# One PSUM bank shared by three tiles, one mask product per chunk, ReLU on ScalarE, and a third expert buffer

## The chip, the cores and the metric

The kernel runs on one core of a Trainium2 chip. The metric is device microseconds for one execution. An execution is timed several times, and one further execution is profiled.

## The reference

The kernel computes three layers in float32 one after the other.

```
linear attention   4 batches, 8 heads, 768 steps, head width 48
    y[t]  = r[t] (state + u k[t] v[t]^T);   state = w state + k[t] v[t]^T
soft MoE           3072 tokens x 384, 8 experts with 4 slots each, hidden 1024
    logits = x phi;  d = softmax over tokens;  slots = d^T x
    slots of expert e:  max(slot w1[e], 0) w2[e];   out = softmax over slots (logits) @ slot_out
feed-forward       3072 tokens x 384, hidden 2048
    h = x w_in;  g = ELU(h);  out = g w_out
```

## The kernel before

The order of the instructions on each engine is the order in which the program is written (a manual schedule); semaphores are set by a layer that tracks tiles, and for PSUM it treats two accesses of one tile in one bank as dependent even where their columns differ, if they come from different engines.

**Attention.** The 3072 tokens are cut into 24 chunks of 128 (six per batch). The loop at L888 runs s from -2 to 23 and works on four chunks at once: chunk s+1 gets its state update `update` (TensorE, into `pu`), its scores `scores` (16 products into two PSUM tiles `ps_a`, one for each half of the heads), the causal mask product `causal` (VectorE, two instructions of 128x512, one ahead of and one behind the product `rT` of `turn_r`), and its bonus term (`bonus_a` into `ps_b`, `bonus_c` a ScalarE copy, `bonus_b` a transpose into `ps_c`, `bonus_d` the ScalarE copy `bs`). Chunk s gets its output rows `rows_a`, `rows_b` and the transpose `x_T` into `ps_x`. Chunk s+2 gets `turn_k`: four transposes into `ps_k`, a ScalarE copy to `kT`, and later the VectorE product `qd` (`cross`). Chunk s+3 gets `turn_r`: four transposes into `ps_r`, then the VectorE product `rT`. At the end of a step `before` (L637) multiplies the running state into `py`, except for the first chunk of a batch (s = 5, 11, 17).

The 8 banks of PSUM are dealt to pools (L406): `pt` 2 (for `ps_r`, `ps_x`, `ps_k`, in this order in each step), `pa` 2, `py` 1, `pu` 1, `pm` 2 (for `ps_b`, `ps_c`, and the MoE's `ps_l`, `ps_e`, `ps_s`). Between these, `extra()` (three per step) runs one stage of the MoE's logits and slot sums for each four chunks, and `wide_a` to `wide_d` turn pieces of the feed-forward weights from 64 to 32 bits in the steps s = 0 to 19.

**Transfers.** Nearly all are issued by SyncE in program order: in each step the next k and v rows, a piece of the wide weights, every second step r, and, every 20/9 steps from s = 2 on, one expert weight (1.5 MB in four transfers, `load_we`). v of a chunk has four buffers; `update` is the first to read it.

**End of attention and experts.** `last_part` (L773) ends the slot sums: `ps_e` transposes, the VectorE copy `et`, the sums `ps_s`, the VectorE products `pl`, the TensorE products `pi`, and `si`, the slots' input. Then `up` (48 products, ReLU by VectorE at L1052), `turn` (transposes into `ph` buffers, copied by ScalarE to `h1T`), `turn_c_a` and `turn_c_b` (the combine weights, split into two parts and transposed), `down`, and `turn_so`. Expert weights 11 and 12 are loaded into room that attention leaves, 13 to 15 into buffers that `up(0)` leaves. Then the feed-forward layer runs to the end, in 48 units.

Of the kernel before, what the change touches and what calls it, by code (L numbers as in the profile page):

```python
# [236 lines left out]
def kernel(  # L237
# [156 lines left out]
    si = const.tile([128, KD, 32], F32, name="si")  # L394
# [3 lines left out]
    with ExitStack() as actx:  # L398
# [164 lines left out]
        pu = pu_p.tile([128, HP, D], F32, name="pu")  # L563
        nc.vector.memset(pu, 0.0)

# [11 lines left out]
        def scores(n, p):  # L577
            if p == 0:
                aps[:] = [pa_p.tile([128, HP, 128], F32, tag="pa", name="ps_a") for a in range(2)]
            for a in range(2):  # L580
                q = slice(64 * a, 64 * a + 64)
                nc.tensor.matmul(out=aps[a][:, p, :], lhsT=kT[q, p, :], rhs=rT[n][q, p, :], start=True, stop=True)  # L582

        def causal(n, a):
            am[n, a] = at2.tile([128, HP, 128], F32, tag="am", name="am", bufs=3)
            nc.vector.tensor_tensor(  # L586
                out=am[n, a], in0=aps[a], in1=mask.unsqueeze(1).to_broadcast([128, HP, 128]), op=ALU.mult
            )
# [29 lines left out]
        def bonus_b(n):  # L618
            pb = pm_p.tile([128, 128], F32, tag="pm", name="ps_c")
# [31 lines left out]
        def rows_a(n, p):  # L651
            c, py = n % NC, pyd[n]
            for a in range(2):
                h = 2 * p + a

                for q in range(0, C, 64):
                    nc.tensor.matmul(  # L657
                        out=py[q:q + 64, h, :], lhsT=am[n, a][:, p, q:q + 64], rhs=vd[n][:, h, :],
                        start=(c == 0), stop=(c == 0 or h == H - 1),
                    )  # L660
            if p == HP - 1:
                am.pop((n, 0)), am.pop((n, 1))
# [225 lines left out]
        for s in range(-2, NCH):  # L888
# [42 lines left out]
            if nxt:  # L931
                causal(s + 1, 1)
# [46 lines left out]
    mid = main.enter_context(tc.tile_pool(name="mid", bufs=1, reuse_waits="tile"))  # L979
# [22 lines left out]
    rm = ea.tile([128, NCH // CG, CG], F32, name="rm")  # L1002
    rs = ea.tile([128, NCH // CG, CG], F32, name="rs")
# [19 lines left out]
    sel = ea.tile([128, 2, NS], F32, name="sel")  # L1023
# [15 lines left out]
    so = [ea.tile([128, DM], F32, name=f"so{a}") for a in range(2)]  # L1039

    def up(a):
        for f in range(2):
# [9 lines left out]
            nc.vector.tensor_scalar(out=h1[a, f], in0=ph, scalar1=0.0, scalar2=None, op0=ALU.max)  # L1052
# [11 lines left out]
    def down(a):  # L1064
        po = po_p.tile([128, DM], F32, tag="po", name="pd")
        for j in range(KF):
            for q in range(4):
# [3 lines left out]
                )  # L1071
        for kk in range(KD):
# [69 lines left out]
    sT = mid.tile([128, KD, 64], F32, name="sT")  # L1142
# [323 lines left out]
```

## Time and profile before

| what | us |
|---|---|
| three timed runs | 440.98, 440.31, 435.86 |
| their median | 440.31 |
| the profiled execution, timed | 437.81 |
| its span from first to last instruction | 435.7 |
| attention (to the first `up` product) | 0 to 163.0 |
| experts (to the end of `turn_so`) | 163.0 to 189.0 |
| feed-forward | 189.0 to 435.7 |

In the profiled execution 2.1 us lie outside the span. TensorE is busy for 93% of the span, VectorE for 82%, ScalarE for 62%, GpSimd for 37%. In the rows, PE is TensorE's products and PEld its weight loads, DVE is VectorE, ACT ScalarE, POOL GpSimd; "L533" is a line of the kernel; a bracket at the end of a row tells how long its engine had been idle and whose work ended that. A release is inferred from semaphores.

### The profile page before, as it was taken

What the parts mean: (1) busy time and instruction counts of PE and PEld (TensorE: products, weight loads), DVE (VectorE), ACT (ScalarE), POOL (GpSimd) and SP (SyncE); (2) the same over time, 40 slices, a digit from 0 to 9 for tenths busy, and PEclk for the clock granted to TensorE, in tenths of its full rate; (3) what the DMA queues carried; (4) which work ended last, traced back from release to release, by engine and by line L of the source; (5) the groups of instructions that cost most, each with busy time, mean ns of one, the idle gap of its engine ahead of it and who ended that gap; (6) DMA issues with size and microseconds to landing.
All of it is one profiled execution on the core that took longest, in us unless ns stands there. A gap on an engine that the chain in (4) does not pass through costs nothing.

```text
span 435.7 us, 10350 instructions
## 1 busy us (share of the span) xinstructions
PE 405.5 (93%) x4177; PEld 356.0 (82%) x4177; DVE 357.9 (82%) x573; ACT 269.8 (62%) x496; POOL 160.2 (37%) x170
## 2 busy tenths in 40 slices
PE   6998999799999979988999999999999899999994
PEld 5777778587777853457999999998989889999994
DVE  5898999969999645669889999998988989777762
ACT  3554566546564411647697878776778767767750
POOL 2265666546666207200004513430314125433340
PEclk9999999989999999999999999999999999999998
DMA  8969998999999986900001111110111002111122
GB/s 149 232 159 278 253 240 274 279 286 247 283 298 257 353 281 219 360 5 0 2 0 38 37 38 37 37 42 32 38 36 38 0 2 72 63 48 47 63 74 80
DMA packets 85097, 57.44 MB, mean 132 GB/s; under 512 B 65328, under 2 KB 76848, under 8 KB 85040
## 3 DMA queue, kind: packets, MB, share of 16 engines
q1 hardware_dynamic: 84224, 56.64, 45.1%
q8 instruction: 35, 0.57, 0.5%
q14 instruction: 22, 0.18, 0.1%
q10 hardware_dynamic: 816, 0.05, 0.1%
HBM read 51.96 MB, written 4.72 MB: 130 GB/s over the span
## 4 chain that ended last, share of the span: by engine, by line
PE 67%; DVE 20%; ACT 5%; issue 5%; DMA 2%; DVEq 0%; ACTq 0%; SPq 0%
PE fo L1304 12%; PE fo L1307 12%; PE fo L1305 12%; PE ps_a L582 4%; PE fh L1259 4%; PE py L657 4%; DVE rT L547 3%; DVE ex L1273 3%; DVE ex L1278 2%; PE pd L1068 2%; PE ph L1046 2%; PE py L643 2%; DVE am L586 2%; PE ps_k L533 2%; PE ps_r L533 2%
## 5 line engine op out<-in xcount | busy, mean ns | idle before, releaser
L1304 PE MATMUL fo<-wh,gh 128*128 128x384 f32 x384 | 130.3, 339 | 1.5 <-ACT gh L1286 1.0
L1305 PE MATMUL fo<-wl,gh 128*128 128x384 f32 x384 | 129.7, 338 | 0.0
L1307 PE MATMUL fo<-wh,gl 128*128 128x384 f32 x384 | 125.5, 339 | 3.2 <-DVE gl L1289 3.2
L1273 DVE SCALAR_TENSOR_TENSOR ex<-ex,th 128x1024 f32<-128x1024 f32 (+1 forms) x52 | 61.1, 1174 | 20.5 <-ACT ex L1270 20.3
L1304 PEld LDWEIGHTS fo<-wh,gh 128*128 128x128 f32 x384 | 72.1, 188 | 6.0 <-ACT acc L1241 2.4
L1307 PEld LDWEIGHTS fo<-wh,gl 128*128 128x128 f32 x384 | 71.8, 188 | 4.2 <-DVE gl L1289 4.2
L1267 ACT ACTIVATE th<-fh 128x1024 f32<-128x1024 f32 (+1 forms) x53 | 50.3, 950 | 38.3 <-PE fh L1259 38.3
L1305 PEld LDWEIGHTS fo<-wl,gh 128*128 128x128 f32 x384 | 72.1, 188 | 1.8
L1289 DVE TENSOR_TENSOR gl<-ex,gh 128x1024 fp32r<-128x1024 f32 (+1 forms) x52 | 68.3, 1314 | 1.7 <-ACT gh L1286 1.3
L337 POOL TENSOR_TENSOR cv<-raw,cv 128x384 f32<-128x384 f32 x12 | 19.4, 1618 | 132.4 <-ACT gh L1286 51.2
L1278 DVE SCALAR_TENSOR_TENSOR ex<-ex,fh 128x1024 f32<-128x1024 f32 (+1 forms) x52 | 58.8, 1131 | 0.5 <-ACT ex L1270 0.4
L1270 ACT ACTIVATE ex<-fh 128x1024 f32<-128x1024 f32 (+1 forms) x53 | 50.3, 949 | 9.6 <-DVE gl L1289 9.2
L1286 ACT CAST gh<-ex 128x1024 fp32r<-128x1024 f32 (+1 forms) x52 | 51.4, 988 | 6.3 <-DVE ex L1278 4.9
L1246 POOL TENSOR_TENSOR acc<-os,acc 128x384 f32<-128x384 f32 x20 | 27.0, 1361 | 43.7 <-ACT os L1245 43.7
L631 POOL TENSOR_TENSOR bv<-vd,bs 128x384 f32<-128x384 f32 x24 | 24.5, 1021 | 39.6 <-ACT bs L626 38.9
L586 DVE TENSOR_TENSOR am<-ps_a,mask 128x512 f32<-128x512 f32 x48 | 32.5, 680 | 2.0 <-PE ps_a L582 1.9
L1259 PE MATMUL fh<-cT,mst 128*128 128x512 f32 x96 | 30.5, 398 | 1.8 <-DVE mst L1186 1.1
L582 PE MATMUL ps_a<-rT,kT 64*128 64x128 f32 x384 | 28.3, 288 | 0.3 <-ACT kT L556 0.3
L657 PE MATMUL py<-vd,am 128*64 128x48 f32 x768 | 27.7, 226 | 0.4 <-DVE am L586 0.4
L657 PEld LDWEIGHTS py<-vd,am 128*64 128x64 f32 x768 | 25.4, 142 | 0.9 <-DVE am L586 0.7
L556 ACT COPY kT<-ps_k 128x512 f32<-128x512 f32 x24 | 14.1, 586 | 18.8 <-PE ps_k L533 18.8
L582 PEld LDWEIGHTS ps_a<-rT,kT 64*128 64x128 f32 x384 | 23.8, 190 | 1.7 <-ACT kT L556 0.4
(166 smaller groups left out, 650.9 us busy)
## 6 DMA issues: line engine op xcount, KB each, us to landing
we<-in_moe_w_dram SPq DMA_DIRECT2D x14, 768.0 KB, 7.6
we<-in_moe_w_dram SPq DMA_DIRECT2D x16, 512.0 KB, 6.4
rw<-in_r_dram SPq DMA_DIRECT2D x12, 384.0 KB, 5.0
rk<-in_k_dram SPq DMA_DIRECT2D x24, 192.0 KB, 4.8
vd<-in_v_dram SPq DMA_DIRECT2D x24, 192.0 KB, 5.4
out_dram<-acc SPq DMA_DIRECT2D x24, 192.0 KB, 1.9
we<-in_moe_w_dram SPq DMA_DIRECT2D x16, 256.0 KB, 5.9
scr<-in_moe_w_out_dram SPq DMA_DIRECT2D x10, 384.0 KB, 5.9
```

The source lines that it names most:

```text
L582: nc.tensor.matmul(out=aps[a][:, p, :], lhsT=kT[q, p, :], rhs=rT[n][q, p, :], start=True, stop=True)
L657: nc.tensor.matmul(out=py[q:q + 64, h, :], lhsT=am[n, a][:, p, q:q + 64], rhs=vd[n][:, h, :], start=(c == 0), stop=(c == 0 or h == H - 1),)
L1259: nc.tensor.matmul(out=ph[n][:, i, :], lhsT=mst[(f + i) // 8][:, 128 * ((f + i) % 8):128 * ((f + i) % 8) + 128], rhs=cT[:, TB * blk:TB * b ...
L1267: nc.scalar.activation(out=th[n][:, s], in_=ph[n][:, s], func=ACTF.Tanh, scale=0.5)
L1270: nc.scalar.activation(out=ex[n][:, s], in_=ph[n][:, s], func=ACTF.Exp)
L1273: nc.vector.scalar_tensor_tensor(out=ex[n][:, s], in0=ex[n][:, s], scalar=1.0, in1=th[n][:, s], op0=ALU.add, op1=ALU.mult)
L1278: nc.vector.scalar_tensor_tensor(out=ex[n][:, s], in0=ex[n][:, s], scalar=0.0, in1=ph[n][:, s], op0=ALU.min, op1=ALU.max)
L1286: nc.scalar.copy(out=gh[n][:, s], in_=ex[n][:, s])
L1289: nc.vector.tensor_tensor(out=gl[n][:, s], in0=ex[n][:, s], in1=gh[n][:, s].bitcast(F32), op=ALU.subtract)
L1304: nc.tensor.matmul(out=o, lhsT=gh[n][:, i, s], rhs=wh, start=(f == first), stop=False)
L1305: nc.tensor.matmul(out=o, lhsT=gh[n][:, i, s], rhs=wl, start=False, stop=False)
L1307: nc.tensor.matmul(out=o, lhsT=gl[n][:, i, s], rhs=wh, start=False, stop=(f == final))
```

## The change

Seven edits, of which the first three belong together:

- PSUM is dealt anew: `pt` 3 banks, `pa` one tile of 2 banks, `py` 1, `pm` 1, and one bank `pub` that holds `pu` (columns 0 to 191), `ps_b` (192 to 319) and `ps_c` (320 to 447).
- `causal` becomes one VectorE instruction of 128x1024 over both halves of the heads, ahead of `rT`; its result has one buffer in place of three.
- The tables `pw` and `vk` lie in buffers of `rT` and `qd`.
- `load_we` starts at s = 1 in place of 2, so the weights 0 to 8 are issued one step earlier.
- Small tiles (`si`, `rm`, `rs`, `sel`, `sT`, `so`) lie in tiles that are done with, and behind attention there is room for three expert weights (11, 12 and 13) in place of two.
- ReLU goes from VectorE to ScalarE.
- `up(1)` is written ahead of `turn_c_a(0)`.

```
-        pt_p = actx.enter_context(tc.tile_pool(name="pt_p", bufs=2, space=PSUM))
-        pa_p = actx.enter_context(tc.tile_pool(name="pa_p", bufs=2, space=PSUM))
+        pt_p = actx.enter_context(tc.tile_pool(name="pt_p", bufs=3, space=PSUM))
+        pa_p = actx.enter_context(tc.tile_pool(name="pa_p", bufs=1, space=PSUM))
...
-        pm_p = actx.enter_context(tc.tile_pool(name="pm_p", bufs=2, space=PSUM))
+        pm_p = actx.enter_context(tc.tile_pool(name="pm_p", bufs=1, space=PSUM))
...
-        pu = pu_p.tile([128, HP, D], F32, name="pu")
+        pub = pu_p.tile([128, 512], F32, name="pub")
+        pu = pub[:, 0:HP * D].rearrange("p (h d) -> p h d", d=D)
         nc.vector.memset(pu, 0.0)
+        psb, psc = pub[:, 192:320], pub[:, 320:448]
...
-        def causal(n, a):
-            am[n, a] = at2.tile([128, HP, 128], F32, tag="am", name="am", bufs=3)
+        def causal(n):
+            am[n] = at2.tile([128, 2, HP, 128], F32, tag="am", name="am", bufs=1)
             nc.vector.tensor_tensor(
-                out=am[n, a], in0=aps[a], in1=mask.unsqueeze(1).to_broadcast([128, HP, 128]), op=ALU.mult
+                out=am[n].rearrange("p a h t -> p (a h) t"), in0=aps[0].rearrange("p a h t -> p (a h) t"),
+                in1=mask.unsqueeze(1).to_broadcast([128, H, 128]), op=ALU.mult,
             )
...
-            pb = pm_p.tile([128, 512], F32, tag="pm", name="ps_b")
+            pb = psb
...
-            pb = pm_p.tile([128, 128], F32, tag="pm", name="ps_c")
+            pb = psc
...
-                causal(s + 1, 0)
+                causal(s + 1)
...
-            if nxt:
-                causal(s + 1, 1)
...
-            if s >= 2 and (s - 2) * (NWE - 1) // NP >= nwe and nwe < NWE - 1:
+            if s >= 1 and (s - 1) * (NWE - 1) // NP >= nwe and nwe < NWE - 1:
...
-    for i in range(nwe, nwe + 2):
-        load_we(i, we2b_p)
+    for i in range(nwe, nwe + 3):
+        load_we(i, we2b_p[i - nwe])
...
-            nc.vector.tensor_scalar(out=h1[a, f], in0=ph, scalar1=0.0, scalar2=None, op0=ALU.max)
+            nc.scalar.activation(out=h1[a, f], in_=ph, func=ACTF.Relu)
...
+    up(1)
     turn_c_a(0)
-    up(1)
```

Three places in the order of the engines. First TensorE in one step of attention, from `ps_r` to the next chunk's state update; before:

```order
L533 MATMUL ps_r<-ident,rp 128x128 [waits PE_49,Activation_49]
L533 MATMUL ps_r<-ident,rp 128x128 x3
L676 MATMUL ps_x<-ident,x 128x128 [waits DVE_49]
L676 MATMUL ps_x<-ident,x 128x128 x2
L620 MATMUL ps_c<-ident,bt 128x128 [waits Activation_49]
L533 MATMUL ps_k<-ident,km 128x128 [waits DVE_49]
L533 MATMUL ps_k<-ident,km 128x128 x3
L643 MATMUL py<-qb_149,rT 64x96 [waits Pool_49]
L643 MATMUL py<-qb_149,rT 64x96 x7
L569 MATMUL pu<-vd,km 48x48 [waits DMAHW7_49]
L569 MATMUL pu<-vd,km 48x48 x7
```

The same place now:

```order
L679 MATMUL ps_x<-ident,x 128x128 [waits DVE_49]
L679 MATMUL ps_x<-ident,x 128x128 x2
L623 MATMUL pub<-ident,bt 128x128 [waits Activation_49]
L533 MATMUL ps_k<-ident,km 128x128 [waits PE_49]
L533 MATMUL ps_k<-ident,km 128x128 x3
L646 MATMUL py<-qb_148,rT 64x96 [waits PE_49,Pool_49]
L646 MATMUL py<-qb_148,rT 64x96 x7
L571 MATMUL pub<-vd,km 48x48 [waits DMAHW7_49,Activation_49]
L571 MATMUL pub<-vd,km 48x48 x7
```

`ps_k` no longer waits for VectorE (its buffer's last reader before was `rT` of the same step), and the state update `pub<-vd,km` now also waits for ScalarE, whose last access of the bank is the copy `bs` out of `ps_c`.

Second, TensorE in `last_part`, from the first `ps_e` transpose to `pi`; before:

```order
L723 MATMUL ps_e<-ident,el 128x128 [waits Activation_49]
L424 MATMUL warm<-ident 128x128 [waits PE_49]
L424 MATMUL warm<-ident 128x128
L739 MATMUL ps_s<-x,et 32x384 [waits DVE_49]
L739 MATMUL ps_s<-x,et 32x384 x3
L723 MATMUL ps_e<-ident,el 128x128 [waits Activation_49]
L424 MATMUL warm<-ident 128x128 x2
L807 MATMUL pi<-rb,pl_2852 128x32 [waits DVE_49]
L807 MATMUL pi<-rb,pl_2853 128x32 [waits DVE_49]
L807 MATMUL pi<-rb,pl_2854 128x32 [waits DVE_49]
```

The same place now:

```order
L726 MATMUL ps_e<-ident,el 128x128 [waits PE_49,Activation_49]
L424 MATMUL warm<-ident 128x128 x2
L742 MATMUL ps_s<-x,et 32x384 [waits DVE_49]
L742 MATMUL ps_s<-x,et 32x384 x3
L726 MATMUL ps_e<-ident,el 128x128 [waits DVE_49,PE_49]
L424 MATMUL warm<-ident 128x128 x2
L810 MATMUL pi<-rb,pl_2731 128x32
L810 MATMUL pi<-rb,pl_2732 128x32
L810 MATMUL pi<-rb,pl_2733 128x32
```

With one `pm` bank the first `ps_e` takes the bank of `ps_l`, whose last reader is the ScalarE copy `el` (`slots_g`), and the second takes that of `ps_s`, whose last reader is the third `pl` product on VectorE; `pi`, behind it, has no wait left of its own.

Third, ScalarE behind attention, from the exponentials of the combine weights on; before:

```order
L1010 ACTIVATE c_sb<-c_sb 128x256 [waits Pool_49] x3
L1120 TENSOR_LOAD flag_i [waits DVE_49]
L1080 CAST cs<-c_sb 128x8x32 [waits Pool_49]
L1062 COPY h1T<-pht 128x512 [waits DVE_49,PE_49]
L1062 COPY h1T<-pht 128x512 [waits PE_49]
```

The same place now:

```order
L1009 ACTIVATE c_sb<-c_sb 128x256 [waits Pool_49] x3
L1051 ACTIVATE h_2839<-ph 128x512 [waits DVE_49,PE_49]
L1051 ACTIVATE h_2854<-ph 128x512 [waits PE_49]
L1120 TENSOR_LOAD flag_i [waits DVE_49]
L1051 ACTIVATE h_2895<-ph 128x512 [waits PE_49]
L1051 ACTIVATE h_2910<-ph 128x512 [waits PE_49,Activation_49]
L1080 CAST cs<-c_sb 128x8x32 [waits Pool_49]
L1061 COPY h1T<-pht 128x512
```

The four ReLUs stand on ScalarE ahead of the first cast `cs` and of `h1T`; the fourth reuses the buffer of the first, which the transposes `pht` read.

## Rows read from the trace of the kernel before

**Rows 1.** Window 40 to 140 us: busy us (count) per engine, TensorE clock, DMA share, GB/s.
```profile
40.00:140.00 100.00, 91.74 (x1740) 76.58 (x1736) 90.38 (x197) 56.88 (x158) 60.70 (x63) 0.98 0.98 267
```

**Rows 2.** Waits of TensorE over the whole span: us in total, times, longest us.
```profile
PE ps_k L533 <- DVE rT L547: 6.8, 18, 0.5
...
PE pu L569 <- DMA vd<-in_v_dram: 2.1, 1, 2.1
...
PE ps_k L533 <- ACT xT L678: 1.4, 3, 0.5
```

**Rows 3.** Timeline of a plain step (start us, us, engine, line, what), TensorE and ScalarE.
```profile
59.99 0.27 PE L620 MATMUL ps_c<-ident,bt 128*128 128x128 f32 x1
...
60.72 0.66 PE L533 MATMUL ps_k<-ident,km 128*128 128x128 f32 x4 [0.45 <-DVE rT L547]
...
61.46 0.59 ACT L556 COPY kT<-ps_k 128x512 f32<-128x512 f32 x1 [0.79 <-PE ps_k L533]
...
61.95 0.17 ACT L626 COPY bs<-ps_c 128x8 f32<-128x8 f32 x1
...
62.01 0.53 PE L569 MATMUL pu<-vd,km 128*48 128x48 f32 x16
```

**Rows 4.** Timeline of TensorE at s = 21, which has no `turn_r`.
```profile
146.16 0.33 PE L620 MATMUL ps_c<-ident,bt 128*128 128x128 f32 x1
146.32 0.60 PE L533 MATMUL ps_k<-ident,km 128*128 128x128 f32 x4
```

**Rows 5.** Timeline of s = 5, a step without `before`.
```profile
49.16 0.66 PE L533 MATMUL ps_k<-ident,km 128*128 128x128 f32 x4 [0.35 <-DVE rT L547]
...
49.91 0.59 ACT L556 COPY kT<-ps_k 128x512 f32<-128x512 f32 x1 [0.69 <-PE ps_k L533]
...
49.97 0.56 PE L569 MATMUL pu<-vd,km 128*48 128x48 f32 x16
...
50.39 0.17 ACT L626 COPY bs<-ps_c 128x8 f32<-128x8 f32 x1
```

**Rows 6.** The page's groups: two VectorE products, 512 and 1024 columns wide.
```profile
L1278 DVE SCALAR_TENSOR_TENSOR ex<-ex,fh 128x1024 f32<-128x1024 f32 (+1 forms) x52 | 58.8, 1131 | 0.5 <-ACT ex L1270 0.4
...
L586 DVE TENSOR_TENSOR am<-ps_a,mask 128x512 f32<-128x512 f32 x48 | 32.5, 680 | 2.0 <-PE ps_a L582 1.9
```

**Rows 7.** Timeline of `last_part`.
```profile
159.13 0.33 PE L723 MATMUL ps_e<-ident,el 128*128 128x128 f32 x1
...
160.03 0.29 DVE L732 COPY et<-ps_e 128x128 f32<-128x128 f32 x1
...
160.23 0.25 ACT L712 COPY el<-ps_l 128x128 f32<-128x128 f32 x1
...
160.38 0.85 PE L739 MATMUL ps_s<-x,et 128*32 128x384 f32 x8 [0.47 <-DVE et L732]
...
161.16 0.33 PE L723 MATMUL ps_e<-ident,el 128*128 128x128 f32 x1
...
161.30 0.86 DVE L752 SCALAR_TENSOR_TENSOR pl<-pall,al,ps_s 128x128 f32<-128x128 f32 x3 [0.70 <-PE ps_s L739]
...
162.66 0.26 DVE L808 COPY si<-pi 128x96 f32<-128x96 f32 x1 [0.37 <-PE pi L807]
```

**Rows 8.** Timeline between `up(1)` and `down(0)`.
```profile
171.60 0.41 ACT L1080 CAST cs<-c_sb 128x256 fp32r<-128x256 f32 x1 [6.00 <-DVE rs L1015]
...
172.78 0.37 DVE L1081 TENSOR_TENSOR cs<-c_sb,cs 128x256 fp32r<-128x256 f32 x1
...
174.17 0.69 DVE L1052 TENSOR_SCALAR h<-ph 128x512 f32<-128x512 f32 x1 [0.42 <-PE pht L1059]
...
174.81 0.66 PE L1088 MATMUL phc<-ident,cs 128*128 128x128 f32 x4 [0.24 <-ACT h1T L1062]
```

**Rows 9.** The window behind the wait for v, columns as in Rows 1.
```profile
87.00:91.00 4.00, 3.54 (x58) 3.45 (x60) 2.02 (x5) 1.28 (x3) 2.42 (x4) 0.57 1.16 276
```

**Rows 10.** Line L525, the loads of v: time from issue to landing.
```profile
DMA to landing us min/median/max: 3.4/5.4/7.8
```

More of the change, by code (lines that the diff above doesn't have):

```diff
@@ L393 @@
     rb = const.tile([GP, 32], F32, name="rb")
-    si = const.tile([128, KD, 32], F32, name="si")
+    si = mask[:, 0:KD * 32].rearrange("p (k c) -> p k c", c=32)
     w2ctx = main.enter_context(ExitStack())
@@ L578, in scores @@
             if p == 0:
-                aps[:] = [pa_p.tile([128, HP, 128], F32, tag="pa", name="ps_a") for a in range(2)]
+                aps[:] = [pa_p.tile([128, 2, HP, 128], F32, tag="pa", name="ps_a")]
             for a in range(2):
                 q = slice(64 * a, 64 * a + 64)
-                nc.tensor.matmul(out=aps[a][:, p, :], lhsT=kT[q, p, :], rhs=rT[n][q, p, :], start=True, stop=True)
-        def causal(n, a):
-            am[n, a] = at2.tile([128, HP, 128], F32, tag="am", name="am", bufs=3)
+                nc.tensor.matmul(out=aps[0][:, a, p, :], lhsT=kT[q, p, :], rhs=rT[n][q, p, :], start=True, stop=True)
+        def causal(n):
+            am[n] = at2.tile([128, 2, HP, 128], F32, tag="am", name="am", bufs=1)
             nc.vector.tensor_tensor(
-                out=am[n, a], in0=aps[a], in1=mask.unsqueeze(1).to_broadcast([128, HP, 128]), op=ALU.mult
+                out=am[n].rearrange("p a h t -> p (a h) t"), in0=aps[0].rearrange("p a h t -> p (a h) t"),
+                in1=mask.unsqueeze(1).to_broadcast([128, H, 128]), op=ALU.mult,
             )
         def bonus_a(n):
-            pb = pm_p.tile([128, 512], F32, tag="pm", name="ps_b")
+            pb = psb
             q = qd.pop(n)
@@ L598, in bonus_c @@
             bt = at2.tile([128, 128], F32, tag="bt", name="bt", bufs=1)
-            nc.scalar.copy(out=bt, in_=misc.pop(n)[:, 0:128])
+            nc.scalar.copy(out=bt, in_=misc.pop(n))
             misc[n] = bt
@@ L661, in rows_a @@
             if p == HP - 1:
[L662 removed]
+                am.pop(n)
         def rows_b(n):
@@ L988, in half @@
         return ht_p.tile([128, 1024], dtype, tag="ht", name=name)
-    we2b_p = w2ctx.enter_context(tc.tile_pool(name="we2b_p", bufs=2, side="right", reuse_waits="tile"))
+    we2b_p = [w2ctx.enter_context(tc.tile_pool(name=f"we2b{i}", bufs=1, side="right", reuse_waits="tile")) for i in range(3)]
     ectx = ExitStack()
-    ea = ectx.enter_context(tc.tile_pool(name="ea", bufs=1, reuse_waits="tile"))
     e2 = ectx.enter_context(tc.tile_pool(name="e2", bufs=2, reuse_waits="tile"))
-    for i in range(nwe, nwe + 2):
-        load_we(i, we2b_p)
+    for i in range(nwe, nwe + 3):
+        load_we(i, we2b_p[i - nwe])
     for h in range(2):
-        for i in range(nwe + 2, 2 * E):
+        for i in range(nwe + 3, 2 * E):
             load_we(i, we_p, h)
     CG = 8
-    rm = ea.tile([128, NCH // CG, CG], F32, name="rm")
-    rs = ea.tile([128, NCH // CG, CG], F32, name="rs")
+    rm = pall[:, 192:192 + NCH].rearrange("p (b c) -> p b c", c=CG)
+    rs = pall[:, 224:224 + NCH].rearrange("p (b c) -> p b c", c=CG)
     sh = [128, CG, NS]
@@ L1038 @@
     h1, h1T, cs = {}, {}, {}
-    so = [ea.tile([128, DM], F32, name=f"so{a}") for a in range(2)]
+    so = {}
     def up(a):
```

12 lines of the change are left out of this document (6 added, 6 removed).

## The prediction

> **What bounds the kernel now.** I read the windows first, for the stage that the change touches most: in 40 to 140 us TensorE is busy 91.7 of 100 us and VectorE 90.4, and the DMA share is 0.98 [rows 1]. So attention is bound by TensorE and VectorE in a ring, with transfers close behind, and not by one engine. Then the waits of TensorE: the largest is `ps_k` waiting for the VectorE product `rT`, 18 times, 6.8 us; three more times `ps_k` waits for the ScalarE copy `xT`, 1.4 us; v comes late once, 2.1 us [rows 2]. Both waits of `ps_k` are for a bank: `ps_r`, `ps_x` and `ps_k` take turns in two, so the third must wait until the first or second has been read. The timeline of a step shows it: `ps_c` starts at 59.99, `ps_k` only at 60.72, 0.73 us later [rows 3]; at s = 21, where there is no `ps_r`, it starts 0.16 us later [rows 4]. The same step shows what comes next: the copy `kT` starts 0.74 us after `ps_k`, the copy `bs` 0.49 us after that, and the state update `pu` at 62.01, while `bs` (61.95, 0.17 us) is still running [rows 3]. That overlap is possible because `pu` and `ps_c` lie in different banks.
>
> **The change, part by part.** Times are for the profiled execution, 437.81 us.
>
> *Third `pt` bank: -10.0 us.* `ps_k` finds a bank whose readers ended a step ago. The bounds: the idle time by the table is 8.2 us [rows 2]; by starts, 0.73 - 0.16 = 0.57 us for the step shown [rows 3, 4]. That step is one of the longest, with 0.45 us of idle by its row, against 8.2 / 21 = 0.39 on average; the starts give 0.12 more than the idle time, so 21 x (0.39 + 0.12) = 10.7 at most. I take 10.0. What covers the next thing: with `ps_k` freed, TensorE would be late for VectorE next where VectorE lags, but VectorE has 9.6% of the time idle [rows 1], and nothing that TensorE needs within the same step comes from `rT`.
>
> *One bank for `pu`, `ps_b`, `ps_c`: +5.4 us.* The update now waits for ScalarE's `bs`, as the order shows. In a plain step `bs` ends 0.74 + 0.49 + 0.17 = 1.40 us after `ps_k` starts [rows 3]; with 0.05 us for the semaphore the update starts 1.45 us or a little more after it, against 1.29 now (60.72 to 62.01): 0.16 to 0.24, I take 0.20. Of the 22 steps s = 0 to 21, three (s = 9, 13, 21) have the `ps_e` transposes in between, 0.3 us [rows 7], and lose nothing. Three more (s = 5, 11, 17) have no `before` between `ps_k` and the update. At s = 5 the update starts 0.81 us after `ps_k`, and `bs` ends 1.40 after it: 0.64 with the semaphore [rows 5]. That holds for s = 5 and 17, which have `ps_e`; s = 11 has not, so its update is ready 0.3 earlier and loses some 0.9. The sum is 16 x 0.20 + 2 x 0.64 + 0.9 = 5.4. Bounds: 0, if ScalarE comes to `kT` earlier than the rows show, and 6.3, at 0.24 each with 0.7 and 1.0 for the three. So a wait replaces the one removed, at half its size. The other accesses of the shared bank (`t` and `bt`) come when the engine named has been done for long.
> The Trainium skill, "PSUM — Partial Sum Buffer", section "PSUM bank collisions raise a hardware error", says that two engines must not touch one bank in the same quadrant of partitions at the same time, different columns and reads against reads included, so that a program has to guard by bank. It speaks against packing three tiles into one bank. The row where `bs` and `pu` overlap is from two banks, so no run here shows the collision itself; by the rule the wait is needed and the two parts sum to -4.6, and without it they would sum to -10.0.
>
> *One mask product: 0.* Two of 512 columns become one of 1024. They stand at 680 ns each, a 1024-column product at 1131 ns mean [rows 6], so VectorE gains up to 0.2 us a step, but `rT` now comes behind all of it. No term for TensorE hangs on either: the scores wait for the mask product of the step before, and `rT` is used a step later. Ends: -4.8, 24 x 0.2, if VectorE were the bound throughout, and 0, since a loss needs `rT` within its own step.
>
> *Fewer `pm` banks in `last_part`: +1.9 us.* All of it is on the path. The first `ps_e` must wait until `el` has been copied out of `ps_l`: 160.23 + 0.25 = 160.48 in place of 159.13. It ends 0.33 later, so `et` starts at 160.87 in place of 160.03, where VectorE's own copies had held it, and `ps_s` 0.85 us later [rows 7]. The second `ps_e` must wait for the third `pl`: 161.30 + 0.86 + 0.85 = 163.01. From `ps_e` to `si` it is 161.16 to 162.66 = 1.50 us, so `si` comes at 164.5 in place of 162.66: +1.9. Bounds 1.0 (if only the first wait counts) and 2.5.
>
> *ReLU and the new place of `up(1)`: +0.5 us.* The first two ReLUs and the third are covered by products. The fourth waits for the transposes `pht` of the first, as it does now (it starts at 174.17 behind `pht`); the cast `cs` (0.41) and VectorE's part (0.37) now come behind it. A ScalarE copy of this size takes 0.59 us [rows 3], the ReLU on VectorE 0.69 [rows 8]. So `phc` starts between 173.9 and 174.2 + 0.59 + 0.41 + 0.37, at 175.3 to 175.5, in place of 174.81: +0.5 to +0.7, and some may be caught up by the transposes behind. Bounds 0 and 0.8.
> The Trainium skill, "ScalarE: Activation LUTs", section "Rules for kernel authors", wants `relu` on VectorE, up to about three times faster per element there in bf16. The rows are fp32 out of PSUM and say the reverse, 0.59 against 0.69. By the rule's factor on the VectorE row, an estimate, the fourth ReLU would take 2.07 us and the sum would be 1.5 higher.
>
> *Third expert buffer: 0.* Weight 13 is loaded without waiting for `up(0)`. TensorE has no wait on an expert weight in the list of its waits, so there is nothing to gain; SyncE's queue is not waited for there. *Earlier weights: 0 to +3.8 each.* A late v cost 2.1 us of idle time and then a clock of 0.57 in the 4 us behind it, half rate for most of it, which is 0.43 x 4 = 1.7 more [rows 2, 9]. v lands 5.4 us after its issue, at most 7.8 [rows 10]. One more or one less of these is as likely as not, so 0. *Tables and small tiles in other buffers: 0*, their readers are done on the same engine or long before.
>
> Sum: -10.0 + 5.4 + 1.9 + 0.5 = -2.2 us. The profiled execution stands 2.5 us below the median of the three timed runs (440.31), which spread over 5.1 us. I set the sum against the mean of all four, 438.7: **436.5 us**.
>
> **The rivals.**
> 1. *The new waits are hidden* (15%): `bs` comes early enough or TensorE would have waited there anyway. Then -10.0 + 2.4 = -7.6, 431.1. For it: ScalarE is busy only 56.9 of 100 us. Against: `bs` stands right behind `kT`, which needs all of `ps_k`.
> 2. *Transfers set the pace* (22%): the DMA share is 0.98 [rows 1], and steps that are 0.2 us shorter ask for more. Then attention gains nothing and the 2.4 us behind it stay: 441.1. Against: v was late only once.
> 3. *Slower: the earlier weights make v late* (13%). Place: the load of v right behind a weight, needed two to three steps later, in the short steps s = 5, 11, 17; with weights at s = 4, 10 and 15 all three now fall shortly before such a step. Price 3.8 us each; two more give 436.5 + 7.6 = 444.1. It decides from the point where v is issued less than 7.8 us before its update [rows 10].
> 4. *The change doesn't do what it says* in one part: the third expert buffer has no wait to remove. This is in the sum already.
>
> **How the numbers follow.** The forecast, 433 to 440, has 50%, the rivals 15, 22 and 13. The range from 431 to 443 leaves out about half of rivals 1 and 3 and a little on both sides. A measurement of this kernel can tell about 2%, 8.8 us. Faster by more than that is below 431.5, which needs rival 1 without any late v: 7%. Slower by more, above 449, would need three or more late v: 2%. The rest, 91%, is within 2%.
>
> **What would show it.** In the profile of the changed kernel: no wait of `ps_k` for `rT` or `xT`, and `ps_k` 0.2 us or less behind `ps_c`; the state update waiting for `bs`, 0.2 us in a plain step and over 0.6 at s = 5; steps shorter by 4.6 / 22 = 0.2 us on average; `si` 3.3 us behind the start of `ps_s`, not 2.3; `phc` behind `cs`. The prediction is wrong if the steps shorten by 0.4 us or more, if new waits for v appear, or if TensorE waits at `bonus_a` or the scores for VectorE instead, which would say that VectorE, not TensorE, was the bound.

## The result and the profile after

The changed kernel is slower: 442.63 us median (439.52 to 445.46, 18 runs) against 437.91 (435.86 to 440.98, 18 runs), a ratio of 1.0111 with a 95% interval of 1.0082 to 1.0140. The prediction was 436.5 us, a gain of 2.2 on the 438.7 from which it set out; the time lies inside the range (431 to 443) and the direction is wrong. The profiled execution took 442.53 us against 437.81.

Read the same views as before. First the window of attention, 40 to 140 us, of the changed kernel (columns as in [rows 1]), and TensorE's waits (total us, times, longest):

```profile
40.00:140.00 100.00, 89.01 (x1723) 75.19 (x1720) 96.35 (x183) 57.16 (x158) 57.77 (x64) 1.00 0.98 265
```
```profile
PE pub L571 <- DMA vd<-in_v_dram: 7.8, 5, 2.2
PE pub L597 <- DVE t L612: 3.3, 5, 1.2
PE pub L571 <- ACT bs L629: 2.2, 3, 0.8
PE ps_a L584 <- DVE rT L547: 0.5, 1, 0.5
PE pub L597 <- DVE t L610: 0.3, 1, 0.3
```

The waits of `ps_k` for `rT` and `xT`, 8.2 us in [rows 2], are gone. In their place stand 3.6 us for `t` in the shared bank, 2.2 for `bs`, and 7.8 for v where it was 2.1. VectorE went from 90.4 busy to 96.4, although two of its instructions became one. The forms of VectorE's work in the same window (busy us, mean ns, idle before) say where:

```profile
L588 DVE TENSOR_TENSOR am<-ps_a,mask 128x1024 f32<-128x1024 f32 x16 | 19.4, 1215 | 0.8 <-PE ps_a L584 0.8
L329 DVE SCALAR_TENSOR_TENSOR scr<-scr 128x384 int32<-128x384 int32 x17 | 11.9, 698 | 0.6
L323 DVE TENSOR_SCALAR scr<-scr 128x384 int32<-128x384 int32 x17 | 10.5, 619 | 0.6
L318 DVE TENSOR_SCALAR scr<-scr 128x384 f32<-128x384 f32 x16 | 7.3, 457 | 0.0
```

L318, L323 and L329 are the pieces `wide_b1` to `wide_b3` that prepare the FFN's wide weights; the change does not touch them. In the kernel before they took 408, 361 and 560 ns in this window. A timeline of one step tells why L323 and L329 got slower. First the kernel before, VectorE and GpSimd:

```profile
61.18 0.48 DVE L318 TENSOR_SCALAR scr<-scr 128x384 f32<-128x384 f32 x1
61.69 0.36 DVE L323 TENSOR_SCALAR scr<-scr 128x384 int32<-128x384 int32 x1
62.09 0.56 DVE L329 SCALAR_TENSOR_TENSOR scr<-scr 128x384 int32<-128x384 int32 x1
62.56 0.68 DVE L561 TENSOR_TENSOR qd<-rT,ps_k 128x512 f32<-128x512 f32 x1
...
62.19 1.14 POOL L631 TENSOR_TENSOR bv<-vd,bs 128x384 f32<-128x384 f32 x1 [0.76 <-ACT bs L626]
```

And the changed kernel, the same place:

```profile
61.93 0.70 DVE L547 TENSOR_TENSOR rT<-ps_r,vt 128x512 f32<-128x512 f32 x1
62.52 0.56 DVE L318 TENSOR_SCALAR scr<-scr 128x384 f32<-128x384 f32 x1
63.12 0.87 DVE L323 TENSOR_SCALAR scr<-scr 128x384 int32<-128x384 int32 x1
64.02 0.56 DVE L329 SCALAR_TENSOR_TENSOR scr<-scr 128x384 int32<-128x384 int32 x1
64.50 0.68 DVE L561 TENSOR_TENSOR qd<-rT,ps_k 128x512 f32<-128x512 f32 x1
65.09 0.35 DVE L334 TENSOR_SCALAR scr<-scr 128x384 int32<-128x384 int32 x1
65.36 0.35 DVE L612 TENSOR_TENSOR t<-qc,pub 128x192 f32<-128x192 f32 x1
...
62.84 0.93 POOL L634 TENSOR_TENSOR bv<-vd,bs 128x384 f32<-128x384 f32 x1
...
65.76 0.43 PE L597 MATMUL pub<-qd,uw 128*32 128x128 f32 x8 [0.36 <-DVE t L612]
```

GpSimd's product `bv` began 1.0 us behind L318 before, and ran beside L329 and the cross product `qd`. Now, with `ps_k` no longer held up, `kT`, `bs` and `bv` come sooner against VectorE: `bv` starts 0.32 us behind L318 and lies over L323, which takes 0.87 us instead of 0.36. VectorE's step, from one `t` to the next, is 65.36 - 59.60 = 5.76 us where it was 63.47 - 58.19 = 5.28, and TensorE waits for `t`.

The overlap alone is not new: before, `bv` lay over L329, and L329 still took 0.56 us. What changed is which of the two starts first. In all 16 steps of the window before, L329 started first, by 0.02 to 0.24 us; it kept its 0.56 us and `bv` took 1.00 to 1.22. In the changed kernel `bv` started ahead of L323 or L329 in 11 of 16 steps, by 0.01 to 0.28 us, and that piece took 0.87 to 1.24 us; in the other five L329 was first again, took 0.56, and `bv` 0.97 to 1.18. L318's mean is another matter: it is 485 ns in a run without `bv` too (e13 below).

Behind attention the rows that answer to [rows 7] (timeline), and the clock of the two stretches (columns as in [rows 1]):

```profile
159.02 0.29 DVE L704 TENSOR_REDUCE al<-ps_l 128x1 f32<-128x128 f32 x1 [2.05 <-PE ps_l L692]
...
161.56 0.33 PE L726 MATMUL ps_e<-ident,el 128*128 128x128 f32 x1 [1.50 <-ACT el L715]
...
164.20 0.45 PE L726 MATMUL ps_e<-ident,el 128*128 128x128 f32 x1 [1.08 <-DVE zr L758]
...
165.30 1.33 PE L810 MATMUL pi<-rb,pl 128*128 128x32 f32 x6
166.66 0.26 DVE L811 COPY mask<-pi 128x96 f32<-128x96 f32 x1 [2.47 <-PE pi L810]
...
166.97 7.01 PE L1045 MATMUL ph<-we,mask 128*32 128x512 f32 x48 [0.35 <-DVE mask L811]
...
179.13 1.09 PE L1058 MATMUL pht<-ident,h 128*128 128x128 f32 x8
...
181.49 0.63 PE L1088 MATMUL phc<-ident,cs 128*128 128x128 f32 x4 [1.26 <-DVE cs L1081]
...
182.92 0.52 PE L1067 MATMUL pd<-we,h1T 128*32 128x384 f32 x2
```
```profile
160.00:165.00 5.00, 2.43 (x18) 1.57 (x18) 2.34 (x13) 1.01 (x6) 0.00 (x0) 0.85 1.07 385
165.00:170.00 5.00, 4.65 (x25) 2.29 (x27) 1.31 (x5) 1.26 (x3) 2.41 (x7) 0.50 1.07 373
```

The copy of the indicator (now a part of `mask`, written `mask<-pi`; `si<-pi` before) starts 7.64 us behind the reduction; it was 4.67 (157.99 to 162.66). From 165 to 170 us the granted clock is 0.50, the 1.2 GHz level, behind a stretch in which TensorE was busy 2.43 of 5 us. So the first 48 `up` products take 7.01 us where they took 5.36. The table adds this up, from the two timelines, each of one execution:

| point | before, us | after, us | added |
|---|---|---|---|
| reduction at the end of attention | 157.99 | 159.02 | +1.03 |
| from there to the copy from `pi` | 4.67 | 7.64 | +2.97 |
| from the copy to the last `pht` ahead of `phc` | 10.82 | 12.47 | +1.65 |
| from there to the first `pd` | 2.79 | 3.79 | +1.00 |
| from `pd` to the end of the span | 259.4 | 257.9 | -1.5 |

The five are the +5.1 of the spans (435.7 to 440.8). The variants of the changed kernel below whose expert weights are not moved behind attention take 257.9 to 258.7 from `pd` to the end, so the last row holds beyond one execution. No run takes the third expert buffer away alone; whether the gain is its doing is open.

### The profile page after: what moved, and what is told of

Its sections match the earlier page's. It is cut to its first block, busy times and chain, and to the rows that moved or that the text cites. A ratio compares the mean times of both kernels' runs of the same rounds, so it can differ in the third digit from the quotient of the medians.

```text
span 440.8 us, 10346 instructions
## 1 busy us (share of the span) xinstructions
PE 404.2 (92%) x4177; PEld 354.6 (80%) x4177; DVE 361.9 (82%) x545; ACT 272.8 (62%) x500; POOL 157.4 (36%) x170
## 4 chain that ended last, share of the span: by engine, by line
PE 61%; DVE 17%; DMA 10%; issue 6%; ACT 5%; SPq 0%; DVEq 0%; ACTq 0%
PE fo L1304 11%; PE fo L1307 11%; PE fo L1305 11%; DMA vd<-in_v_dram 9%; PE fh L1259 4%; PE py L660 3%; DVE ex L1278 3%; DVE ex L1273 3%; PE ph L1045 3%; PE ps_a L584 3%; PE pd L1067 2%; PE py L646 2%; PE ps_r L533 2%; PE pub L571 2%; PE ps_k L533 1%
## 5 line engine op out<-in xcount | busy, mean ns | idle before, releaser
L588 DVE TENSOR_TENSOR am<-ps_a,mask 128x1024 f32<-128x1024 f32 x24 | 29.2, 1217 | 2.6 <-PE ps_a L584 2.6
L634 POOL TENSOR_TENSOR bv<-vd,bs 128x384 f32<-128x384 f32 x24 | 21.6, 899 | 23.8 <-ACT bs L629 23.5
L613 POOL TENSOR_TENSOR qc<-t,w 128x192 f32<-128x192 f32 x20 | 14.1, 703 | 44.0 <-DVE t L612 24.4
L660 PE MATMUL py<-vd,am 128*64 128x48 f32 x768 | 26.7, 222 | 0.0
L681 ACT COPY xT<-ps_x 128x384 f32<-128x384 f32 x24 | 11.5, 479 | 22.6 <-PE ps_x L679 22.4
```

What stands on the lines that cost most here:

```text
L660: nc.tensor.matmul(out=py[q:q + 64, h, :], lhsT=am[n][:, a, p, q:q + 64], rhs=vd[n][:, h, :], start=(c == 0), stop=(c == 0 or h == H - 1),)
```

## The experiments

Each ratio is to the kernel before, with its 95% interval; the changed kernel stands at 1.0111 [1.0082, 1.0140]. "Steps" are the 17 state updates from the one at about 45 us to the last: 102.90 us before (44.88 to 147.78), 103.75 in the changed kernel (45.06 to 148.81). They are read from one profiled execution each, and late transfers move them: e3 and e4, whose attention is the changed kernel's, took 108.79 and 103.28, with four waits for v each (9.1 and 5.9 us in all). Differences of 1 us in them say nothing where transfers come late.

**One part at a time.** Expert weights asked for one step later again:
```
- if s >= 1 and (s - 1) * (NWE - 1) // NP >= nwe and nwe < NWE - 1:
+ if s >= 2 and (s - 2) * (NWE - 1) // NP >= nwe and nwe < NWE - 1:
```


> The changed kernel with the expert weights issued from s = 2 again, as before the change. The changed kernel waits for v 5 times, 7.8 us, where the kernel before waits once, 2.1 us. Theory A, the earlier weights made v late: one wait for v or none is left, and with 3.8 us for each that goes the time falls by 5 us or more from 442.6, to 437 or less. Theory B, the steps that are 0.45 us shorter where nothing stops them ask more of the transfers than these give, wherever the weights stand: 4 to 6 waits for v are left and the time stays within 1.5 us of 442.6.

Measured: 441.77 us, 1.0055 [1.0020, 1.0090]. Neither theory came out whole: one wait for v of 0.3 us is left (in an execution of 444.82 us), as A said, but the time is near B's. Its waits for `t` are 6.5 us where the changed kernel had 3.6. v loaded one step earlier:
```
- vd[n] = at2.tile([128, H, D], F32, tag="vd", name="vd", bufs=4)
+ vd[n] = at2.tile([128, H, D], F32, tag="vd", name="vd", bufs=5)
- if 2 <= s + 3 < NCH: load_v(s + 3)
+ if 2 <= s + 4 < NCH: load_v(s + 4)
```


> The changed kernel with v issued one step earlier, into five buffers. Theory C, v is only issued too late for a landing of 5 to 9 us: the five waits for v go, and with them 7.8 us of idle time and the half clock behind, so that the time is 433 to 437. Theory B, the transfers as a whole set the pace: the wait moves to another transfer (k, or the wide pieces on VectorE and GpSimd), and the time stays at 441 to 444.

Measured: 440.42 us, 1.0041 [1.0008, 1.0074], above what theory C gave. No wait for v is left, but `t` and `bs` take over, not another transfer as B had it; its waits:
```profile
PE pub L597 <- DVE t L612: 6.0, 12, 1.2
PE pub L571 <- ACT bs L629: 2.8, 4, 0.8
PE pub L597 <- DVE t L610: 1.2, 2, 0.9
```
By the two ratios the late v was worth some 3 us of time, not the 5.7 that its wait grew by. In the last part, the order mended so that the second `ps_e` does not wait for the third `pl`:
```
  slots_b(j)
+ slots_g(j)
  combine_a()
  ...
- slots_g(j)
  combine_c(); slots_e(j); slots_f(j)
- slots_c(j, (1,)); warm(2); combine_b()
+ warm(3); combine_b(); slots_c(j, (1,))
  slots_d(j, (1,))
```


> The changed kernel with last_part written for one bank: the copy el directly behind the exponentials and ahead of sc, and the second ps_e transpose behind pi. Theory D, the two new waits there cost 3.0 us up to si and, by the clock that falls to one half behind them, 1.65 us more in up(0): si comes 4.7 to 5.1 us behind the first reduction of the last part (7.6 in the changed kernel), the first 48 products of up take 5.4 us in place of 7.0, and the time falls by 4 to 5 us, to 438. Rival, the clock falls for another reason (the idle time ahead of the last chunk's rows): the products stay at 7.0 us, and 2 to 3 us are gained, to 440.

Measured: 438.24 us, 1.0003 [0.9975, 1.0031]: the largest single effect, 1.1%. In its profile the copy from `pi` is 4.73 us behind the reduction and the first `up` takes 5.36, as theory D said. (That execution took 443.07 us: late v ate the gain, with one wait of 4.6 us.) The ReLU put back on VectorE, and `turn_c_a(0)` ahead of `up(1)`:
```
- nc.scalar.activation(out=h1[a, f], in_=ph, func=ACTF.Relu)
+ nc.vector.tensor_scalar(out=h1[a, f], in0=ph, scalar1=0.0, scalar2=None, op0=ALU.max)
- up(1); turn_c_a(0)
+ turn_c_a(0); up(1)
```


> The changed kernel with ReLU on VectorE again and up(1) behind turn_c_a(0), as before the change. Theory E, the fourth ReLU and the cast behind it on ScalarE hold up phc: the wait of 1.3 us goes, pd starts 2.8 us behind the end of up(1) as before the change in place of 3.8, and the time falls by about 1 us, to 441.6. Rival, the 0.3 us less of VectorE time per ReLU and the relief of VectorE there are worth as much elsewhere: no difference, 442.6.

Measured: 441.84 us, 1.0069 [1.0042, 1.0096]. The intervals of this and the changed kernel overlap, so the gain in time is not certain; the profile shows the mechanism: no wait of `phc` for `cs`, and from `pht` to `pd` 2.80 us, as before.

**Is it VectorE?** v earlier, and GpSimd's `bv` out of the way, so that the bonus term is left unscaled:
```
- bv = at2.tile([128, H, D], F32, tag="bv", name="bv", bufs=1)
- nc.gpsimd.tensor_tensor(out=bv, in0=vd[n], in1=bs...to_broadcast(...), op=ALU.mult)
- bsb[n] = bv
+ bsb[n] = vd[n]
```


> The changed kernel with v loaded a step earlier (five buffers), and GpSimd's product bv of the bonus left out: TensorE adds v itself in its place, so the bonus is not scaled (this part of the result is left out). GpSimd then does nothing in the attention steps beside VectorE's wide pieces. Theory F (VectorE's two-input pieces of L323 and L329 are slowed by GpSimd's product running beside them, VectorE then sets the step, and TensorE waits for t in the shared bank): the mean of L323 falls from about 650 ns to about 360 and that of L329 from about 730 to about 560, VectorE is free some 0.5 us per step, the wait of L597 for t goes under 2 us in all, the step is 5.2 to 5.4 us, and the time is 425 to 432 us. Rival G (the pieces are slower because of the one wide mask product or of what TensorE and ScalarE do beside them, not because of GpSimd): L323 and L329 stay above 600 and 680 ns, the steps stay 5.8 to 6.4 us, and the time is 438 to 442 us.

Measured: 440.21 us, 1.0016 [0.9979, 1.0052]. L323 fell to 360 ns and L329 to 561, the wait for `t` to 1.2 us, all as theory F says; the time did not follow (F had 425 to 432), and the steps took 102.56 us. e2, which differs from it by `bv` alone, took 101.99. So the slowing is GpSimd's, but something else held the kernel. ScalarE's timeline has it:

```profile
91.98 0.27 ACT L713 COPY el<-ps_l 128x128 f32<-128x128 f32 x1 [0.33 <-DVE al L702]
96.23 0.55 ACT L314 ACTIVATE scr<-scr 128x384 f32<-128x384 f32 x1 [3.98 <-DMA scr<-in_moe_w_out_dram]
96.67 0.54 ACT L315 ACTIVATE scr<-scr 128x384 f32<-128x384 uint32 x1
97.11 0.25 ACT L602 COPY bt<-pub 128x128 f32<-128x128 f32 x1
```
ScalarE stands 3.98 us waiting for a wide weight that has not landed; `bt` and TensorE wait behind it. In the list of ScalarE's waits such weights cost 14.4 us here, 6.5 in the changed kernel, 1.8 before.

**Is it the transfers?** The ten expert weights moved behind attention, in both kernels:
```
- load_we(nwe, we_p)
  nwe += 1
  ...
  last_part(GS - 1)
+ for i in range(NWE): load_we(i, we_p)
```


> The changed kernel with the ten expert weights that are loaded beside the attention steps put behind attention, so that the steps share the queue with r, k, v and the FFN's wide weights alone. The whole result is computed; its total time says nothing, since the expert weights are late; only the attention steps between 40 and 140 us count. Theory I (with the third turn buffer the transfers of 26 MB in these 100 us set the pace: v or the wide weights are late whatever the engines do): no wait for v, ScalarE is not late with bt by more than 1 us, the DMA share falls well under 0.9, and the steps are 5.2 to 5.9 us, the reduction 3 to 6 us earlier than in the run with earlier v if VectorE is not the next bound. Theory F' (VectorE full with the slowed wide pieces is the bound of the step even with no late transfer): the steps stay at 5.8 to 6.4 us with waits of L597 for t of 5 us or more, as in the run with earlier v, and the reduction is within 1.5 us of it.

> The kernel before with the same ten expert weights put behind attention: only the attention steps count. Theory I: before waits for rT in nearly each step and not for transfers, so the wait for v of 2.1 us goes and the steps stay at 5.7 to 6.3 us; the attention of the changed kernel with no expert weights is then 4 to 8 us shorter than this one, which is what the third turn buffer gives once nothing is late. Theory F': the two differ by less than 2 us.

> The changed kernel with GpSimd's product bv left out (the bonus is not scaled: this part of the result is left out) and with the ten expert weights put behind attention; only the attention steps count. VectorE is then not slowed and no transfer is late. Theory F' (VectorE's slowed pieces are the bound of the changed attention once nothing is late): the 17 steps from the one at 45 us to the last take 96 to 99 us in place of 102.2 in the changed kernel with no experts and 99.1 in the kernel before with no experts, and the waits for t fall from 7.9 us to under 2. If the shared bank's waits for t and bs have a cause other than VectorE's delay, the steps stay within 1 us of 102.2.

> The changed kernel with two turn buffers again in place of three, all else as changed (the eighth bank is left unused), and the expert weights behind attention; only the attention steps count. My prediction gave the third buffer 10 us. Theory F': VectorE is the bound in the changed steps, so the third buffer is worth little there: the 17 steps take 102 to 104 us, as TensorE's wait for rT (5 to 7 us) comes back and the wait for t goes. If the buffer is worth what I predicted, they take 109 us or more.

In e14 `pt_p` has `bufs=2`. The total times (466.51, 467.26, 456.12 and 469.50 us) count the late weights. The window 40 to 140 us of the four, in the order e9, e10, e13, e14:
```profile
40.00:140.00 100.00, 91.82 (x1764) 76.25 (x1760) 98.76 (x184) 57.14 (x159) 56.99 (x64) 1.00 0.66 154
```
```profile
40.00:140.00 100.00, 93.58 (x1810) 78.11 (x1808) 92.92 (x202) 58.61 (x164) 63.21 (x65) 1.00 0.66 155
```
```profile
40.00:140.00 100.00, 98.04 (x1926) 83.74 (x1926) 94.38 (x192) 60.76 (x172) 45.44 (x49) 1.00 0.70 168
```
```profile
40.00:140.00 100.00, 91.56 (x1737) 75.20 (x1734) 92.75 (x182) 57.09 (x159) 56.77 (x63) 1.00 0.65 154
```
and the steps, first and last state update from the timelines:

| kernel | first, us | last, us | 17 steps | steps with the weights there |
|---|---|---|---|---|
| e10, before | 46.44 | 145.54 | 99.10 | 102.90 |
| e9, changed | 45.14 | 147.38 | 102.24 | 103.75 |
| e14, changed, two turn buffers | 46.05 | 149.50 | 103.45 | not run |
| e13, changed, no `bv` | 43.46 | 137.02 | 93.56 | 102.56 (e5) |

Each of the four was executed once. Theory I expected e9 3 to 6 us ahead; theory F', that it stays behind VectorE. F' holds: with nothing late VectorE is busy 98.76 of 100 us, and the changed attention is 3.1 us *longer* than the one before, more than the 2 us that F' allowed. The two pieces in e9, then in e13:
```profile
L329 DVE SCALAR_TENSOR_TENSOR scr<-scr 128x384 int32<-128x384 int32 x17 | 13.4, 786 | 0.6
L323 DVE TENSOR_SCALAR scr<-scr 128x384 int32<-128x384 int32 x17 | 11.3, 667 | 0.6
```
```profile
L329 DVE SCALAR_TENSOR_TENSOR scr<-scr 128x384 int32<-128x384 int32 x16 | 9.0, 560 | 0.9
L323 DVE TENSOR_SCALAR scr<-scr 128x384 int32<-128x384 int32 x16 | 5.8, 360 | 0.6
```
They lose 226 + 307 ns a step in e9, 9.1 us in 17 steps, which is about the 8.7 us between e9 and e13. The third buffer is worth 103.45 - 102.24 = 1.2 us there: without it TensorE waits for `xT` (5.5 us) and `rT` (3.1), L323 and L329 are at 360 and 562 ns, and the wait for `t` is 0.5. e14 has the one mask product and `bv` and its pieces are not slowed, so it takes the third buffer too, by what that makes earlier. The rest of the change in attention, the shared bank and the one mask product above all, costs 103.45 - 99.10 = 4.4 us (e14 against e10). With `bv` gone TensorE goes at its own pace, 98.04 busy, and the kernel is 5.5 us ahead of the one before, beyond the 96 to 99 us that F' gave. That faster pace is of no use once the expert weights are back: e5, which has them and v one step earlier, took 102.56, 9.0 us more, at a DMA share of 0.97. So both theories are right in part: VectorE and the transfers each hold the changed attention near 102 to 104 us, and removing one alone finds the other.

**Can the order be had without the overlap?** `cross` ahead of all wide pieces (with v earlier), then with last part and ReLU mended as in e3 and e4, then with `bonus_d` also ahead of `turn_k`:
```
+ if ahead: cross(s + 2, ps)
  for f in (wide_b1, wide_b2, wide_b3): wide(s, f)
- if ahead: cross(s + 2, ps)
```


> The changed kernel with v a step earlier, and VectorE's cross product (which reads PSUM) moved ahead of the three wide pieces of its step, so that the wide pieces come later against GpSimd's product; all else as changed, the whole result is computed. Theory F: the overlap is smaller, so L323 comes nearer to 400 ns and the steps get shorter by 0.2 to 0.4 us; the time is 433 to 438 us. Rival G: the pieces keep their times, the order alone changes nothing or delays the next mask product, and the time is 440 to 444 us.

> The kernel with the cross product first and v a step earlier, and with the last part's order mended as in the run of the last part, and the ReLU put back on VectorE. If the parts add up as they did one by one (the last part 1.1% and the ReLU 0.4% of the time, each timed alone), it is 6 to 7 us faster than the same kernel without these two: 427 to 432 us if theory F holds there, 433 to 437 us if the cross product first gives nothing. If the last part's gain lay in the same half-clock stretch as the ReLU's, the two together give 4 to 5 us.

> As the kernel with cross product, v, last part and ReLU mended, and ScalarE and VectorE asked for the next step's bonus ahead of the turned keys, so that bs and t are there earlier. Theory F with the shared bank as what TensorE waits for: the waits of L597 for t and L571 for bs, some 6 + 3 us in all in the run with earlier v, fall by more than half, and the time is 3 to 5 us under that kernel. Rival H (VectorE is full, so what comes earlier in its queue only puts something else later): the waits move to rT or xT of the turned keys by as much, and the time is within 2 us of that kernel.

Measured: e6 444.09 us, 1.0121 [1.0076, 1.0166]; e7 438.85, 1.0003 [0.9974, 1.0033]; e8 437.24, 0.9954 [0.9920, 0.9988]. L323 and L329 were at 360 and 559 ns in e6, but VectorE now stood idle for 7.7 us ahead of `cross`, 6.7 of them for `kT`: one loss for another, and e6 missed its 433 to 438. Last part and ReLU together gave 1.2%; apart they had given 1.5, which the intervals do not tell from it. e7 missed its 427 to 437, and e8 is within 2 us of it, as rival H said: the wait for `bs` went, but TensorE waited 11.2 us for `t`. Next, VectorE's order as in the change, with v, last part and ReLU, then also `bonus_d` first:

> The changed kernel with v a step earlier, the last part's order mended and the ReLU on VectorE; VectorE's pieces in the order of the change. Each alone gave 0.7, 1.1 and 0.4% against the changed kernel: if they add up, 432 to 434 us, a ratio to before of 0.986 to 0.992. If v's earlier place and the mended end give the same microseconds (what is gained in attention is waited for by the expert weights behind it), the ratio is 0.995 to 1.0.

> As the kernel with v, last part and ReLU, and in addition bs and its bonus product asked for ahead of the turned keys. If the wait for bs (0.8 us, three or four times) and the wait for t behind it cost time, this is 1 to 3 us faster than that kernel; if GpSimd's product, which then starts earlier, only lies otherwise against VectorE's wide pieces, the two are within 1 us.

Measured: e11 437.11 us, 0.9980 [0.9955, 1.0006]; e12 436.49, 0.9954 [0.9933, 0.9976]. The parts did not add up: the sum of the three was 0.989, though the intervals of the four ratios that make it up leave it uncertain by some 0.008, nearly the whole shortfall. ScalarE waited 9.1 us for wide weights in e11, and its 17 steps took 104.76. Last, `cross` behind the first wide piece, which fills the wait for `kT`; the same with `bonus_d` first; and that with the expert weights one step later:
```
- for f in (wide_b1, wide_b2, wide_b3): wide(s, f)
+ wide(s, wide_b1)
  if ahead: cross(s + 2, ps)
+ for f in (wide_b2, wide_b3): wide(s, f)
```


> The changed kernel with v a step earlier, last part and ReLU mended, and VectorE's cross product put between the first and the second of the wide pieces: the first fills the 0.5 us in which the cross product waits for kT, the others come later against GpSimd's product. Theory F': L323 and L329 fall below 500 and 600 ns with no new idle time ahead of the cross product, VectorE is free again by 0.3 us a step, and the time is 1 to 4 us under that of the kernel with v, last part and ReLU alone (437.1). If the transfers, which fill 0.98 of this stretch, set the pace whatever VectorE does, the time is within 1 us of it and ScalarE's or TensorE's waits for a DMA grow.

> The same with bs and its product asked for ahead of the turned keys, so that GpSimd's product begins earlier and has ended when the second wide piece comes. Theory F': L323 and L329 are at about 360 and 560 ns, L318 above 450, and the time is 0 to 2 us under the kernel with the cross product second. If transfers set the pace, the two are within 1 us.

> As the kernel with the cross product second, bonus ahead, v earlier, last part and ReLU, and with the expert weights asked for one step later, as in the kernel before. If the transfers set the pace of attention, fewer of them by one weight (512 to 768 KB, 1.9 to 2.9 us at 265 GB/s) lie ahead of v and the wide weights in the middle of attention, ScalarE's waits for the wide weights fall, and the time is 1 to 3 us under 435.6. If they only have to come behind attention, the time is within 1 us of it.

Measured: e15 437.24 us, 0.9962 [0.9933, 0.9992]; e16 435.63, 0.9934 [0.9909, 0.9959]; e17 435.04, 0.9922 [0.9890, 0.9955]. e15 is level with e11, and ScalarE's waits for wide weights grew to 13.2 us, the sign that was named for the transfers. In e16 `bv` (67.03, 0.95 us) lies over L318 and `cross`, and L323 and L329 are back at their own pace:
```profile
66.73 0.56 DVE L318 TENSOR_SCALAR scr<-scr 128x384 f32<-128x384 f32 x1
67.46 0.69 DVE L561 TENSOR_TENSOR qd<-rT,ps_k 128x512 f32<-128x512 f32 x1 [0.17 <-ACT kT L556]
68.06 0.35 DVE L323 TENSOR_SCALAR scr<-scr 128x384 int32<-128x384 int32 x1
68.45 0.56 DVE L329 SCALAR_TENSOR_TENSOR scr<-scr 128x384 int32<-128x384 int32 x1
...
67.03 0.95 POOL L634 TENSOR_TENSOR bv<-vd,bs 128x384 f32<-128x384 f32 x1
```
VectorE's busy time in the window fell to 90.63, yet the steps still take 102.41 us, and ScalarE waits 10.0 us for wide weights in all. That points to the transfers; no run of e16 has the expert weights moved away, so it is not shown. e17 is within 1 us of e16, so one weight more or less in front decides nothing that can be measured. (Its expectation took the size of one transfer for a weight; a weight is 1.5 MB in all.) Both beat both kernels: e17 is 0.8% under the one before and the changed kernel is 1.1% over it.

## Why the prediction was wrong

**Third `pt` bank, -10.0, and one shared bank, +5.4.** On TensorE's side the sum was of the right sign: with VectorE at its own pace and nothing late, e13 (which lacks `bv`) is 5.5 us shorter than e10 over 17 steps, where the two terms came to -4.6 over 22, or -3.6 over 17. The step that failed is the cover: "VectorE has 9.6% of the time idle, and nothing that TensorE needs within the same step comes from `rT`". VectorE's spare time is not fixed. Freeing `ps_k` moves `bs`, and with it GpSimd's `bv`, ahead of VectorE's wide pieces, which cost 0.40 us more a step in the means of L323 and L329 alone (258 + 138 ns in the changed kernel). So the third bank, -10.0 over 22 steps or -7.7 over 17, gave -1.2 in e9 against e14. I did not look at what a sooner `bs` would start on GpSimd.

**"The other accesses of the shared bank (`t` and `bt`) come when the engine named has been done for long."** False: `bonus_a` writes the bank that `t` reads, so a late VectorE now stops TensorE, for 3.6 us in the changed kernel and 7.9 in e9. This is one of the signs of being wrong that the prediction named, and new waits for v another. TensorE's wait for `bs` is listed at only 2.2 us in three places; but all of the change in attention without the third bank cost 4.4 us over 17 steps (e14 against e10), near the 4.2 that +5.4 over 22 makes. How that splits between the shared bank and the mask product was not tested.

**Transfers.** Rival 2 said that attention then gains nothing, and gave 441.1; the steps went from 102.90 to 103.75. I put 22% on it with a DMA share of 0.98 in hand; "v was late only once" was weak evidence, since what is late is also ScalarE's wide weights, which I had not read. Rival 3 was right in its mechanism (five waits for v in place of one; 0.3 us of them left in e1) and too dear: 441.77 with the weights back and 440.42 with v earlier, by their ratios 2.4 and 3.1 us under the changed kernel.

**Mask product, 0.** Not tested alone. VectorE gained nothing by it: 1215 ns against two of 680 that follow at 0.60 us from start to start.

**`last_part`, +1.9.** The waits cost what was worked out: in e2, e4, e5, e6 and e9 the copy from `pi` comes 6.56 to 6.58 us behind the reduction, 1.9 more than before. What failed is that it ended there. In the changed kernel the clock was at 0.50 in 165 to 170 us, which adds 7.64 - 6.57 = 1.07 us up to the copy and 1.65 in the first `up`. With the waits gone e3 has neither. Of the nine profiles with these waits, five have the drop (the changed kernel, e1, e5, e9 and e14) and four have not (e2, e4, e6 and e13); of the eight with the order mended none has it. So the drop goes with the waits, but not in each execution; what decides it stays open. [rows 9] had shown such a drop behind a wait, and I priced it for v alone.

**ReLU, +0.5.** Mis-sized: 1.0 us from `pht` to `pd`, beyond the bound of 0.8. The fourth ReLU and the cast came in the order that I gave; VectorE's part of `cs` took 0.53 us where the sum had 0.37, and the transposes behind caught up next to nothing.

**Third expert buffer, 0.** Perhaps a gain of about 1 us, the last row of the table; not tested alone.

So the forecast had a gain of 4.6 in attention that VectorE and the transfers took away, and a loss of 2.4 behind it that measured 5.6 in the profiled execution. That 442.63 lies inside the range is due to the range's width, not to the mechanism.

## What to carry to other kernels

A wait that is removed makes everything behind it earlier: follow the earlier start on *each* engine, GpSimd too, and look at what it will then run beside and which of the two will start first, because an engine's free time shrinks when its instructions get slower. Where two limits lie within a few per cent of each other (here VectorE and the transfers), take one away at a time in an experiment in which the other is absent, or neither will show. Packing tiles into one bank joins the engines that touch it: list every reader and writer of the bank, and treat each as a wait.

## What the runs showed of the hardware

Where a VectorE piece that reads and writes SBUF alone met GpSimd's product `bv` of 128x384, the one that started second paid. L329 took 0.56 us in every step of the kernel before, where it started 0.02 to 0.24 us ahead of `bv`, and `bv` took 1.00 to 1.22 us. In e9 `bv` started 0.07 to 0.28 us ahead of L323 or L329 in every step of the window; that piece took 0.87 to 1.15 us (0.36 and 0.56 without), and `bv` 0.83 to 0.92. In e6, where `bv` meets neither, it took 0.83. VectorE's product `qd`, which has one operand in PSUM, kept its 0.68 us where `bv` had started 0.20 to 0.45 us ahead of it. The Trainium skill, "SBUF — State Buffer", section "Who interferes with whom", says that VectorE and GpSimd share a pair of SBUF ports, that a VectorE instruction with two SBUF inputs meets a GpSimd instruction that reads SBUF there, and that `tensor_scalar` can too in a mode with two ports. This agrees with the rows of L329, which has two SBUF inputs, and with the return of L323 and L329 to 360 and 560 ns without `bv`; that L323, a `tensor_scalar`, runs in that mode is not shown by a row.
